# Merging two first-layer matmuls into one of 512 columns in 51 product pairs, and three more splits per chunk on GpSimd

## The chip, the core and the metric

One core of a Trainium2 chip runs the whole program. Its engines run side by side, each through its own queue in order, and wait for each other by semaphores: TensorE (PE in the profile; its weight loads are PEld), VectorE (DVE), ScalarE (ACT), GpSimd (POOL) and SyncE (SP), which issues nearly all transfers. The metric is the time of one execution in microseconds (us) on the device; lower is better. Matmuls read SBUF and write PSUM; a bank of PSUM holds 512 float32 columns.

## The reference

```python
# attention per batch and head (8 x 8), 576 tokens, head size 64, 128 random features
q_p, k_p = phi(q * scale), phi(k * scale)     # exp(x @ omega.T - |x|^2/2 - max) / sqrt(128)
x = (q_p @ (k_p.T @ v)) / (q_p @ k_p.sum(0) + 1e-6)   # then heads side by side: 8 x 576 x 512
# token mixing and MLP
u = x + mix(x)                                # x.T @ U @ V over the 576 tokens, rank 32
out = u + np.maximum(u @ w_ch1, 0.0) @ w_ch2  # 512 -> 2048 -> 512
```

Nothing is rounded on purpose: the result is asked for in the precision of float32. The change lies in the last line alone, in `u @ w_ch1`.

## The kernel before

**Stages.** Attention and mixing fill the first 400 us or so. Then comes the MLP over 4608 tokens, which are 36 tiles of 128. They are taken in nine chunks (`c`): chunk 0 has six tiles, chunks 1 to 7 have four (512 tokens), chunk 8 has two. Chunks 0 and 8 go through `whole1`, a plain matrix product, and the change does not touch them.

**Pairs.** In chunks 1 to 7 the first layer is computed in eight pairs (`p` = 0 to 7). Pair `p` makes two column blocks of `u @ w1`, `p` and `p + 8`, 128 columns each, for 512 tokens. Weights and tokens are cut into 2 x 2 blocks (halves of the 512 inputs; two column blocks, two halves of 256 tokens), and the 2 x 2 product is made with seven block products in place of eight, from sums and differences of the blocks. `products` issues them in the order (X, Y, Z, X, Y, W, Z), which names the PSUM bank that each accumulates into: product 3 goes on top of product 0 in X, product 4 on top of 1 in Y, product 6 on top of 2 in Z. So a bank has to be read between its two products. The text counts products from 0 to 6.

**High and low parts.** Matmuls run on `fp32r`, and each operand is kept as a high part and the rest (`split`: ACT casts the high part, another engine subtracts it). A product of 256 inputs is two steps `k` of 128, and each step three passes: high weights by high tokens, high weights by low tokens, low weights by high tokens. That is 7 x 2 x 3 = 42 matmuls of 256 columns a pair (L958).

**What reads them.** `after(i)` issues, after product i, what turns the banks into the hidden layer. `sums` is one DVE step (L771). Before the change: after product 0, ACT copies X to `p1` (L935); after 1, `u2 = Y + p1`; after 3, `relu` of X; after 4, `u3 = Y + p1`, then `c22 = Z + u3` and its `relu`; after 5, `c21 = W + u3` and its `relu`; after 6, `c12 = Z + u2` and its `relu`. `relu` is one ACT step for the high part of `g` (L916) and one DVE step for the low part (L918). The tiles are called `near` (`p1`, `u2`, `u3`, `c21`) and `far` (`c22`, `c12`) in the profile, the banks `p_s`.

**The second layer in between.** The 24 matmuls of 512 columns that take a pair's `g` into the output (L984, `second`) are handed out one at a time by `take` between the first-layer matmuls of the next pair: one between two products (`between`), two inside products 1, 3 and 5 and three inside the others. Results of a chunk are added to `u` and stored by `store` (DVE L1005, then SP) from `between`, one after each product, in the first pair of the next chunk.

**The next chunk.** In pairs 5 and 6 DVE transposes the tokens of the next chunk (L855), GpSimd makes their sums (L872, tile `us`), and in pair 7 `Chunk.add` splits the seven operands (L767 ACT, L768 the rest; tiles `ux`, `uy`): the first ahead of the pair, the others after products 0 to 5, DVE subtracting except for operands 3 and 5 of chunk 1. In chunk 1 the pairs also make the weight operands of the pairs that follow, from sums on DVE (`ws`) and splits on ACT and GpSimd (`wx`); from chunk 2 on these are read back from memory.

Names such as `keep` hold each engine's queue to the order of the program text.

## Time and profile before

| | |
|---|---|
| median of 3 runs | 1090.22 us (1090.05 to 1092.08) |
| profiled execution | 1088.64 us, of it the span of the core's instructions 1086.9 us |
| granted TensorE clock, mean | 0.996 |
| busy | PE 99%, PEld 90%, DVE 61%, ACT 46%, POOL 31% |
| chain that ended last | PE 84%, DVE 5%, ACT 3%, issue 2%, POOL 2% |
| L958, first-layer matmuls | 1728 + 624 |
| L984, second-layer matmuls | 1728 |

The page gives busy time by engine, the span in 40 slices, the chain of work that ended last, and groups of equal instructions with the mean time of one. A matmul's duration in the rows contains time in which the next one already runs, so what a matmul costs is read from one start to the next.

```profile
PE   9999999999999999999999999999999999999998
DVE  4689998998977776655733634634643643643421
POOL 3247547556445556565200100100100100100143
```

These are tenths of busy time in 40 slices of 27 us: the pairs of chunks 2 to 7 lie in about slices 20 to 38, where DVE has room and POOL has little to do.

### The profile page before, as it was taken

Reading aid. Unit: us, or ns where it says so; the run is one execution under the profiler, and the core shown is the slowest. Engines: PE = TensorE matmul, PEld = TensorE weight load, DVE = VectorE, ACT = ScalarE, POOL = GpSimd, SP = SyncE. Lnnn points to the kernel's source line nnn. Section 1 sums busy time; section 2 is a strip of 40 time slices with the busy share of each in tenths; the row PEclk is TensorE's granted clock in tenths of the full one; section 3 lists DMA queues with packets and bytes.
Section 4 is the critical chain, followed back from the end, with each engine's and each line's share of the span. In section 5 each row is a group of like instructions: output and inputs, shape, how many; then the busy total and the mean of one; then the engine's idle time right before and its main releaser. Section 6 shows DMA issues by size and latency. Waiting matters only on the chain.

```text
span 1086.9 us, 20562 instructions
## 1 busy us (share of the span) xinstructions
PE 1075.8 (99%) x7119; PEld 975.5 (90%) x7119; DVE 665.8 (61%) x1460; ACT 502.6 (46%) x1417; POOL 334.0 (31%) x345
## 2 busy tenths in 40 slices
PE   9999999999999999999999999999999999999998
PEld 8889999999988888898898989999888888888887
DVE  4689998998977776655733634634643643643421
ACT  5789989899856664343311312311321311311232
POOL 3247547556445556565200100100100100100143
PEclk9899999999999999999999999999999999999999
DMA  8688787787224453565776875875885785775510
GB/s 135 131 160 145 169 171 150 160 176 122 88 78 146 146 146 97 185 223 193 254 217 173 246 225 156 257 229 158 233 255 168 222 253 163 223 246 157 181 59 20
DMA packets 344583, 187.93 MB, mean 173 GB/s; under 512 B 276128, under 2 KB 276128, under 8 KB 344480
## 3 DMA queue, kind: packets, MB, share of 16 engines
q1 hardware_dynamic: 342112, 186.32, 63.3%
q8 instruction: 57, 0.93, 0.4%
q10 hardware_dynamic: 2368, 0.30, 0.2%
q14 instruction: 46, 0.38, 0.1%
HBM read 152.99 MB, written 33.55 MB: 172 GB/s over the span
## 4 chain that ended last, share of the span: by engine, by line
PE 84%; DVE 5%; ACT 3%; issue 2%; POOL 2%; DMA 1%; SPq 1%; POOLq 0%; DVEq 0%; ACTq 0%
PE p_s L958 25%; PE p_n L984 17%; PE p_q L984 15%; PE p_p L907 5%; PE p_n L494 4%; PE p_kv L448 4%; PE p_p L536 3%; PE p_p L537 2%; PE p_p L538 2%; PE p_q L474 2%; PE py L331 2%; POOL mag L168 1%; DVE mag L147 1%; ACT e L551 1%; DVE mag L144 1%
## 5 line engine op out<-in xcount | busy, mean ns | idle before, releaser
L958 PE MATMUL p_s<-ux,wx 128*128 128x256 f32 x1728 | 364.0, 280 | 0.4 <-DVE far L771 0.3
L958 PEld LDWEIGHTS p_s<-ux,wx 128*128 128x128 f32 x1728 | 321.6, 188 | 31.5 <-DVE far L771 0.6
L984 PE MATMUL p_n<-w2h,g 128*128 128x512 f32 x576 | 219.3, 395 | 0.0
L984 PE MATMUL p_q<-w2h,g 128*128 128x512 f32 x512 | 195.3, 392 | 0.0
L551 ACT ACTIVATE e<-p_p,nm 128x128 f32<-128x128 f32 x576 | 166.9, 389 | 25.0 <-DVE nm L544 16.3
L958 PE MATMUL p_s<-uy,wx 128*128 128x256 f32 x624 | 132.6, 279 | 0.0
L417 POOL TENSOR_TENSOR xl<-xT,xh 128x384 fp32r<-128x384 f32 x95 | 94.4, 1011 | 119.7 <-ACT xh L413 92.5
L958 PEld LDWEIGHTS p_s<-uy,wx 128*128 128x128 f32 x624 | 117.1, 188 | 11.1
L916 ACT ACTIVATE g<-far 128x256 fp32r<-128x256 f32 x112 | 46.8, 418 | 169.5 <-DVE far L771 169.5
L872 POOL TENSOR_TENSOR us<-uT 128x512 f32<-128x512 f32 x14 | 19.0, 1357 | 338.1 <-DVE uT L855 338.1
L984 PEld LDWEIGHTS p_n<-w2h,g 128*128 128x128 f32 x576 | 108.6, 189 | 9.3
L984 PE MATMUL p_n<-w2l,g 128*128 128x512 f32 x288 | 113.4, 394 | 0.0
L544 DVE TENSOR_REDUCE nm<-p_p 128x4 f32<-128x512 f32 x144 | 97.8, 679 | 25.1 <-PE p_p L538 17.1
L771 DVE TENSOR_TENSOR near<-p_s,near 128x256 f32<-128x256 f32 x168 | 70.4, 419 | 67.9 <-PE p_s L958 66.4
L768 POOL TENSOR_TENSOR wx<-w1f,wx 128x256 fp32r<-128x256 f32 x86 | 68.1, 807 | 135.2 <-DMA u<-u_dram 81.4
L918 DVE SCALAR_TENSOR_TENSOR g<-p_s,g 128x256 fp32r<-128x256 f32 x56 | 23.7, 423 | 138.6 <-ACT g L916 138.6
L916 ACT ACTIVATE g<-p_s 128x256 fp32r<-128x256 f32 x56 | 21.5, 383 | 184.8 <-PE p_s L958 184.8
L984 PEld LDWEIGHTS p_q<-w2h,g 128*128 128x128 f32 x512 | 96.2, 188 | 9.9
L984 PE MATMUL p_q<-w2l,g 128*128 128x512 f32 x256 | 100.7, 393 | 0.0
L536 PE MATMUL p_p<-omh,xh 128*128 128x256 f32 x288 | 93.2, 324 | 1.4 <-ACT e L551 0.9
L907 PE MATMUL p_p<-ux,wx 128*128 128x512 f32 (+1 forms) x480 | 84.5, 326 | 0.2 <-DVE g L918 0.2
L918 DVE SCALAR_TENSOR_TENSOR g<-far,g 128x256 fp32r<-128x256 f32 x112 | 49.5, 442 | 53.7 <-ACT g L916 53.7
(133 smaller groups left out, 2061.4 us busy)
## 6 DMA issues: line engine op xcount, KB each, us to landing
wx<-wx_dram SPq DMA_DIRECT2D x336, 256.0 KB, 3.2
raw<-in_moe_w_ch_dram SPq DMA_DIRECT2D x32, 512.0 KB, 4.0
wx_dram<-wx SPq DMA_DIRECT2D x56, 256.0 KB, 2.3
u_dram<-x SPq DMA_DIRECT2D x36, 256.0 KB, 2.1
u<-u_dram SPq DMA_DIRECT2D x34, 256.0 KB, 4.2
out_dram<-u SPq DMA_DIRECT2D x34, 256.0 KB, 3.2
kt<-in_k_dram SPq DMA_DIRECT2D x120, 72.0 KB, 2.7
qt<-in_q_dram SPq DMA_DIRECT2D x120, 72.0 KB, 2.6
```

Source lines behind the costliest of these rows:

```text
L417: rest.tensor_tensor(out=self.xl[-1], in0=self.turned, in1=f32(self.xh[-1]), op=ALU.subtract)
L448: tc.keep_in_program_order(nc.tensor.matmul(o, e[:, h, :], w, start=(s == 0 and h == 0), stop=(s == NT - 1), skip_group_check=True))
L536: nc.tensor.matmul(o, part.xh[g][:, ts], oh, start=True, stop=False)
L544: nc.vector.tensor_reduce(out=self.nm[:, :n], in_=self.pp[:, :n], axis=AX.X, op=ALU.max, negate=True)
L551: nc.scalar.activation(out=self.e[:, j, :], in_=self.pp[:, j, :], func=AF.Exp, bias=self.nm[:, j : j + 1])
L768: keep(rest.tensor_tensor(out=hl[:, 1], in0=x, in1=f32(hl[:, 0]), op=SUBTRACT))
L771: keep(nc.vector.tensor_tensor(out=out, in0=a, in1=b, op=op))
L907: nc.tensor.matmul(ph, l, r, start=(cc + i == 0), stop=(cc == NC - 1 and i == 2))
L916: keep(nc.scalar.activation(out=g[:, 0, ts], in_=x, func=AF.Relu))
L918: keep(nc.vector.scalar_tensor_tensor(out=g[:, 1, ts], in0=x, scalar=0.0, in1=f32(g[:, 0, ts]), op0=ALU.max, op1=ALU.subtract))
L958: tc.keep_in_program_order(nc.tensor.matmul(o, l, r, start=(i in (0, 1, 2, 5) and k + j == 0), stop=(k == 1 and j == 2), skip_group_check= ...
L984: tc.keep_in_program_order(nc.tensor.matmul(po, l, r, start=(begin and n + i == 0), stop=(end and n == len(fs) - 1 and i == 2)))
```

## The change

In 51 pairs (all eight of chunks 2 to 7, and pairs 2, 3 and 4 of chunk 1; `wide`), the first two passes of each step, which share the high weights, become one matmul whose moving operand is the high and the low tokens side by side: 2 x 256 = 512 columns. The bank is then two halves wide, and the second half holds the product with the low tokens. The third pass goes on top of the first half. A step is two matmuls in place of three, a pair 28 in place of 42. The two halves have to be added: where one instruction read a bank, `whole` and `add` now use one for the first half and a DVE sum for the second. After product 3, `c21` serves as a scratch tile for X. Second-layer matmuls stand at other places inside a product, in the same number.

The other edit moves the subtraction of operands 1, 3 and 5 of chunks 2 to 7 from DVE to GpSimd (chunk 1's 3 and 5 were there already).

```diff
-            split(self.slot(self.ops), x, nc.gpsimd if self.c == 1 and i in (3, 5) else nc.vector)
+            split(self.slot(self.ops), x, nc.gpsimd if i in ((3, 5) if self.c == 1 else (1, 3, 5)) else nc.vector)
...
-            bank = lambda n, b: ps.tile([P, HT], F32, name="p_s", tag=n, bufs=b)
+            bank = lambda n, b: ps.tile([P, 1 + wide, HT], F32, name="p_s", tag=n, bufs=b)
...
+            def whole(to, o):
+                keep(nc.scalar.copy(out=to, in_=o[:, 0]))
+                if wide:
+                    sums(to, o[:, 1], to, ADD)
+
+            def add(to, o, x):
+                sums(to, o[:, 0], x, ADD)
+                if wide:
+                    sums(to, o[:, 1], to, ADD)
...
                 if i == 0:
-                    keep(nc.scalar.copy(out=p1, in_=X))
+                    whole(p1, X)
                 elif i == 1:
-                    sums(u2, Y, p1, ADD)
+                    add(u2, Y, p1)
                 elif i == 3:
-                    self.relu(g[0], t1, X)
+                    if wide:
+                        whole(c21, X)
+                    self.relu(g[0], t1, c21 if wide else X[:, 0])
                 elif i == 4:
                     out()
-                    sums(u3, Y, p1, ADD)
-                    sums(c22, Z, u3, ADD)
+                    add(u3, Y, p1)
+                    add(c22, Z, u3)
                     self.relu(g[1], t2, c22, out)
                 elif i == 5:
-                    sums(c21, W, u3, ADD)
+                    add(c21, W, u3)
                     self.relu(g[1], t1, c21)
                 elif i == 6:
-                    sums(c12, Z, u2, ADD)
+                    add(c12, Z, u2)
                     self.relu(g[0], t2, c12)
...
+                    parts = [(o[:, 0], *lr) for lr in passes((wt[:, 0, k], wt[:, 1, k]), (x[:, 0, k], x[:, 1, k]))]
+                    if wide:
+                        parts[:2] = [(o, wt[:, 0, k], x[:, :, k])]
...
-                        if 3 * k + j in ((1, 3) if i % 2 else (0, 2, 3)):
+                        if n in (((1, 2), (0, 1, 2)) if wide else ((1, 3), (0, 2, 3)))[i % 2 == 0]:
                             take(steps, 1)
...
-            g = now.products(pairs, between, steps, out)
+            g = now.products(pairs, between, steps, out, c > 1 or 1 < p < 5)
```

In the changed kernel the first-layer matmuls are L972, the second layer L999, the copy L934, and `store` L1020.

**TensorE, from the end of product 4 to the start of product 6** in the second pair of chunk 4 (`uy` is the operand of product 4, `ux` that of 5 and 6; `w2h`, `w2l` are second-layer weights). Before:

```order
L958 MATMUL p_s<-uy,wx 128x256 x2
L984 MATMUL p_q<-w2h_5703,g 128x512
L958 MATMUL p_s<-ux,wx 128x256 x2
L984 MATMUL p_q<-w2h_77,g 128x512
L958 MATMUL p_s<-ux,wx 128x256 x2
L984 MATMUL p_q<-w2l_78,g 128x512
L958 MATMUL p_s<-ux,wx 128x256 x2
L984 MATMUL p_q<-w2h_77,g 128x512
L958 MATMUL p_s<-ux,wx 128x256
```

Now:

```order
L972 MATMUL p_s<-uy,wx 128x256
L999 MATMUL p_q<-w2h_5703,g 128x512
L972 MATMUL p_s<-ux,wx 128x512
L972 MATMUL p_s<-ux,wx 128x256
L999 MATMUL p_q<-w2h_77,g 128x512
L972 MATMUL p_s<-ux,wx 128x512
L999 MATMUL p_q<-w2l_78,g 128x512
L972 MATMUL p_s<-ux,wx 128x256
L999 MATMUL p_q<-w2h_77,g 128x512
L972 MATMUL p_s<-ux,wx 128x512
```

Between product 4 and product 6 there stand the same four second-layer matmuls and product 5, now as two matmuls of 512 and two of 256 columns. The last row of each is product 6's first matmul, into Z.

**VectorE, in any pair of chunks 2 to 7 without stores or transposes**, from product 3 to product 5. Before:

```order
L918 SCALAR_TENSOR_TENSOR g<-p_s,g 128x256
L771 TENSOR_TENSOR near<-p_s,near 128x256
L771 TENSOR_TENSOR far<-p_s,near 128x256
L918 SCALAR_TENSOR_TENSOR g<-far,g 128x256
L771 TENSOR_TENSOR near<-p_s,near 128x256
```

Now, from the four sums `p1`, `u2` (two) and `c21` on, whose last is the one after product 3:

```order
L771 TENSOR_TENSOR near<-p_s,near 128x256 x4
L918 SCALAR_TENSOR_TENSOR g<-near,g 128x256
L771 TENSOR_TENSOR near<-p_s,near 128x256 x2
L771 TENSOR_TENSOR far<-p_s,near 128x256
L771 TENSOR_TENSOR far<-p_s,far 128x256
L918 SCALAR_TENSOR_TENSOR g<-far,g 128x256
```

Between the low part of `g` after product 3 and the last read of Z there were two sums and now there are four; the low part of `g` itself now follows a sum and not PSUM alone. On ScalarE one COPY of X stands ahead of the ReLU after product 3.

**GpSimd, from one chunk's sums to the next one's** (the row `us<-uT` follows the transposes in pair 5 or 6; the second `us<-uT,us` is made in pair 7). Before:

```order
L872 TENSOR_TENSOR us<-uT 128x512
L872 TENSOR_TENSOR us<-uT,us 128x512
L872 TENSOR_TENSOR us<-uT 128x512
L872 TENSOR_TENSOR us<-uT,us 128x512
L872 TENSOR_TENSOR us<-uT 128x512
```

Now:

```order
L872 TENSOR_TENSOR us<-uT 128x512
L872 TENSOR_TENSOR us<-uT,us 128x512
L872 TENSOR_TENSOR us<-uT 128x512
L768 TENSOR_TENSOR ux<-us,ux 128x512
L872 TENSOR_TENSOR us<-uT,us 128x512
L768 TENSOR_TENSOR ux<-uT,ux 128x512
L768 TENSOR_TENSOR uy<-us,uy 128x512
```

In pair 7 the low parts of operands 1, 3 and 5 now stand around the sum that follows operand 1; on VectorE the same three rows are gone from that pair. SP's queue is the same but for line numbers.

## The prediction, made before the change was run

> **What bounds the kernel now.** I read the head of the page first, then the table of stretches for the product stage, then who waited for whom on TensorE, and last single rows of the timeline.

> ```profile
> span 1086.9 us, 20562 instructions
> PE 1075.8 (99%) x7119; PEld 975.5 (90%) x7119; DVE 665.8 (61%) x1460; ACT 502.6 (46%) x1417; POOL 334.0 (31%) x345
> 530.00:1030.00 500.00, 500.00 (x3144) 449.84 (x3143) 237.25 (x515) 114.57 (x279) 29.94 (x24) 1.00 0.71 212
> PE p_s L958 <- DVE far L771: 0.3, 1, 0.3
> ```

> TensorE (PE) is busy 99% of the span. The third line is the stretch that holds chunks 2 to 7, 48 of the 51 changed pairs (busy us and count of PE, its weight loads, DVE, ACT, POOL, then the clock): PE is busy 500.00 of 500.00 us at clock 1.00, VectorE (DVE) 237, ScalarE (ACT) 115, GpSimd (POOL) 30. The last line is all that PE waited from 500 to 1033 us: once. So nothing hides behind PE here; every wait put on it is paid in full, and each step off it is gained in full. The sum is made against the profiled execution, 1088.64 us (span 1086.9 and 1.74 around it); the median of the runs is 1.6 higher. A move under 0.2% (2 us) can't be told from none.

> **Part 1, the matmuls.** Each of the 714 merges (51 pairs, 14 each) turns two matmuls of 256 columns, which share their weights, into one of 512. Rows of PE, start and duration:

> ```profile
> 427.01 0.39 PE L984 MATMUL p_m<-w2h,g 128*128 128x512 f32 x1
> ...
> 428.37 4.32 PE L907 MATMUL p_p<-ux,wx 128*128 128x512 f32 x24
> ...
> 1039.24 0.88 PE L907 MATMUL p_p<-uy,wx 128*128 128x256 f32 x6
> 1039.95 0.88 PE L907 MATMUL p_p<-ux,wx 128*128 128x256 f32 x6
> 1040.67 0.40 PE L984 MATMUL p_n<-w2h,g 128*128 128x512 f32 x1
> ```

> The durations overlap, so the price is start to start. Six of 512 columns lie between the first two rows: 1.36/6 = 0.227 us. Twelve of 256 lie in the last three: 1.43/12 = 0.119. Inside a pair, below, a 512 takes 0.23 and two 256 take 0.23 to 0.24. A merge so saves 0.001 to 0.011 us; no row shows a moving operand in two strided halves, so these are its bounds too. I take 0.005, nearer the rows inside a pair: 714 x 0.005 = 3.6 us gained (0.7 to 7.9).

> [...]

> **Part 2, the additional sums.** Each product now leaves two halves. Per wide pair that is one more ACT copy and seven more DVE sums. DVE has room on average (237 of 500), so what counts is order. Product 6 accumulates into Z, so its first matmul has to wait until DVE has read product 2 out of Z, and this read stands behind all of product 4's sums. A normal pair now (chunk 4, second pair), PE, then DVE, then ACT:

> ```profile
> 712.45 0.40 PE L958 MATMUL p_s<-uy,wx 128*128 128x256 f32 x2
> 712.69 0.40 PE L984 MATMUL p_q<-w2l,g 128*128 128x512 f32 x1
> ...
> 714.08 0.40 PE L958 MATMUL p_s<-uy,wx 128*128 128x256 f32 x2
> 714.32 0.40 PE L984 MATMUL p_q<-w2h,g 128*128 128x512 f32 x1
> ...
> 715.95 0.28 PE L958 MATMUL p_s<-ux,wx 128*128 128x256 f32 x1
> ```

> ```profile
> 713.36 0.42 DVE L918 SCALAR_TENSOR_TENSOR g<-p_s,g 128x256 fp32r<-128x256 f32 x1 [3.00 <-ACT g L916]
> 714.51 0.42 DVE L771 TENSOR_TENSOR near<-p_s,near 128x256 f32<-128x256 f32 x1 [0.73 <-PE p_s L958]
> 714.97 0.42 DVE L771 TENSOR_TENSOR far<-p_s,near 128x256 f32<-128x256 f32 x1
> 715.88 0.42 DVE L918 SCALAR_TENSOR_TENSOR g<-far,g 128x256 fp32r<-128x256 f32 x1 [0.48 <-ACT g L916]
> 716.22 0.42 DVE L771 TENSOR_TENSOR near<-p_s,near 128x256 f32<-128x256 f32 x1
> ```

> ```profile
> 712.95 0.38 ACT L916 ACTIVATE g<-p_s 128x256 fp32r<-128x256 f32 x1 [4.12 <-PE p_s L958]
> 715.43 0.42 ACT L916 ACTIVATE g<-far 128x256 fp32r<-128x256 f32 x1 [2.10 <-DVE far L771]
> 718.96 0.37 ACT L935 COPY near<-p_s 128x256 f32<-128x256 f32 x1 [0.54 <-PE p_s L958]
> ```

> Product 3 ends at 712.45 + 0.40 = 712.85, product 4 at 714.48, product 6 starts at 715.95, 3.10 after product 3's end. DVE reads Z at 714.97 and is done at 715.39: 0.56 us to spare today. A DVE step that needs the one before starts 0.46 after it (714.51, 714.97); one that doesn't, 0.34 after it (715.88, 716.22); a step handed from one engine to another starts 0.03 to 0.04 after the end.

> The new chain from product 3's end: ACT copies c21's first half (0.37) 0.04 to 0.41; DVE adds the second (0.42) 0.44 to 0.86; ACT's ReLU (0.42) 0.90 to 1.32; DVE's low part of g starts at 1.35, so u3's first sum at 1.69 (matmuls of product 4 are done by 1.63); then four sums in a chain: 1.69 + 3 x 0.46 = 3.07 for the last, which ends at 3.49. PE gets there at 3.10 less four merges, 3.08. Such a wait stands in the trace once, in the last pair of chunk 1:

> ```profile
> 526.16 0.40 PE L984 MATMUL p_q<-w2h,g 128*128 128x512 f32 x1
> 526.82 0.39 PE L958 MATMUL p_s<-ux,wx 128*128 128x256 f32 x1 [0.27 <-DVE far L771]
> 527.04 0.40 PE L984 MATMUL p_q<-w2h,g 128*128 128x512 f32 x1
> ...
> 526.34 0.42 DVE L771 TENSOR_TENSOR far<-p_s,near 128x256 f32<-128x256 f32 x1
> ```

> DVE ends at 526.76, the matmul starts 0.05 later, and the next one comes 0.22 after it in place of 0.12: 0.10 lost to the restart. So PE starts at 3.54 against 3.08 and pays 0.46 + 0.10 = **0.56 us a pair**. Bounds: 0.35, if the restart costs no 0.10 and each link is a little shorter; 0.66, if ACT's copy starts 0.10 after the matmul as the ReLU at 712.95 does. Behind it the work of products 5 and 6 slips by as much as PE does, so I count no second wait. The other reuses have room: X is read twice before product 3, Y before product 4, each over a microsecond ahead. It is paid in 37 pairs (six in each of chunks 2 to 7, and the last of chunk 7): 20.7 us.

> In the first pair of chunks 2 to 7 the stores of the chunk before stand in the same queue, one ahead of u3:

> ```profile
> 706.97 0.68 DVE L1005 TENSOR_TENSOR u<-p_q,u 128x512 f32<-128x512 f32 x1
> 707.57 0.41 DVE L771 TENSOR_TENSOR far<-p_s,near 128x256 f32<-128x256 f32 x1
> ```

> A store holds DVE 0.60 (706.97 to 707.57): 6 x (0.56 + 0.60) = 7.0 us. Here DVE's 0.60 had the 0.56 of slack as cover; the four sums used that cover up.

> **Part 3, GpSimd.** Three of the seven low parts of the next chunk go from DVE to POOL: 18 in all, off a queue that is late and onto one that idles (30 of 500 us). First single steps of today's last pair of chunk 2, then groups of the page (busy us, mean ns of one):

> ```profile
> 605.29 0.69 DVE L768 TENSOR_TENSOR ux<-us,ux 128x512 fp32r<-128x512 f32 x1
> ...
> 606.23 1.67 DVE L768 TENSOR_TENSOR uy<-us,uy 128x512 fp32r<-128x512 f32 x1
> ...
> 606.06 1.30 POOL L872 TENSOR_TENSOR us<-uT,us 128x512 f32<-128x512 f32 x1 [1.74 <-DVE ux L768]
> ...
> L918 DVE SCALAR_TENSOR_TENSOR g<-near,g 128x256 fp32r<-128x256 f32 x56 | 29.1, 520 | 27.1 <-ACT g L916 27.1
> L767 ACT CAST ux<-us 128x512 fp32r<-128x512 f32 x20 | 11.9, 616 | 0.1
> L771 DVE TENSOR_TENSOR ws<-w1f 128x256 f32<-128x256 f32 x16 | 8.4, 523 | 0.0
> L768 POOL TENSOR_TENSOR ux<-us,ux 128x512 fp32r<-128x512 f32 x1 | 1.7, 1742 | 0.0
> ```

> The rows show a price: the same DVE subtraction of two SBUF operands took 0.69 alone and 1.67 while POOL's 1.30 ran. In the last pair of chunks 2 to 6 POOL now does three of up to 1.74 and one sum of 1.30 besides, 5.2 to 6.5 us of some 12, while DVE does eight steps of this kind (four low parts, four of g). Without meeting: operand 4's low part stands ahead of u3 and needs ACT's 0.62 cast after the ReLU, to 1.94; DVE starts it at 1.97, u3 follows 0.60 later at 2.57 and not 1.69: 0.56 + 0.88 = 1.4 us. With three low parts caught at 0.98 each, 4.3. I take 3.0, in between, since POOL is at work about half the time: 5 x 3.0 = 15.0 us. In the three wide pairs of chunk 1 weight sums (L771 `ws`, 0.52 mean) stand in DVE's queue, and POOL works on weights: 0.56, one sum more (0.40), half of the g steps longer by up to 0.5 (mean 0.52 against 0.42): 3 x 1.4 = 4.2 us (0.6 to 2.0 each). The wait at 526.82 should go, as its pair loses three DVE subtractions: 0.5 us gained.

> No DMA and no store changes its place in SP's queue, so I cost them at nothing: a longer pair only gives the weight tiles' transfers more time to land.

> **Sum.** 20.7 + 7.0 + 15.0 + 4.2 - 0.5 - 3.6 = +42.8 us on 1088.64: 1131.4, and 1133 on the scale of the median.

> **Rivals.**
> - *POOL's parts don't meet DVE's.* The last pairs cost 1.4, those of chunk 1 0.9: 20.7 + 7.0 + 7.0 + 2.7 - 4.1 = 33.3, 1123.5 us. For it: 13 of these subtractions ran at 0.69. Chance 0.16.
> - *They meet throughout and the delay runs on to products 3 and 4*: 4.3 and 2.0 each, +51.1, 1141 us. For it: the row at 606.23. Chance 0.20. [...]
> - *The normal pair's wait is covered*, because I have a link or two too many, and only the queues of first, last and chunk 1 pairs cost: 3.6 + 12.2 + 2.5 - 4.1 = 14.2, 1104 us. Against it: the single row at 526.82 waits in just this place. Chance 0.05.
> - *Faster: nothing waits.* Then only -4.1 is left, 1086 us. It needs the chain of 3.49 to end by 3.03, two of its links gone. Chance 0.03.
> - *Faster: the pairs are paced by weight loads.* PEld is busy 450 of 500 us, and 14 of 66 loads a pair go. At 500/3144 = 0.159 us each that is 113 us: 1024 us. It decides the sign from 0.065 us saved a merge (46.4/714); the rows give 0.011 at most. Chance 0.02. [...]

> **Chances.** The main case has 0.52; 0.02 is left for sums that end within 0.2% by accident. Faster 0.05, same 0.02, slower 0.93. The bounds of all terms give 1109 to 1149; the range 1114 to 1146 takes in the first two rivals and leaves out under 2 in 10.

> **What would show it.** PE's waits: some 50 of `p_s` (now L972) on DVE `far`, 0.4 to 0.5 us each in normal pairs, and L972 PE rows of 512 columns that start 0.23 before the next. A normal pair lasts some 11.0 us in place of 10.5. In last pairs POOL rows `ux<-us,ux` beside DVE rows over 1 us. Wrong if PE's table of waits stays near empty, if the next matmul after a merged one comes under 0.2 us later, or if the waits stand at product 3 or in the second layer.

## The result and the profile after

The changed kernel takes 1135.07 us (median of 4 runs, 1134.84 to 1135.94) beside 1090.13 us for the kernel before (4 runs): 4.25% slower, ratio 1.0425 [1.0407, 1.0443], 44.9 us. The profiled execution of the changed kernel is the one of 1135.94 us.

The page of the changed kernel, its head and TensorE's row of 40 slices; then the stretch 530 to 1075 us (busy us and count of PE, PEld, DVE, ACT, POOL, then the granted clock, DMA share and GB/s); then what PE and its weight loads waited for (us in total, times, longest):

```profile
span 1134.1 us, 19646 instructions
PE 1092.5 (96%) x6405; PEld 944.9 (83%) x6405; DVE 789.1 (70%) x1799; ACT 520.5 (46%) x1468; POOL 359.4 (32%) x363
PE   9989999999999999999999999899899999999998
```

```profile
530.00:1075.00 545.00, 519.47 (x2494) 424.31 (x2493) 354.75 (x834) 131.37 (x328) 51.60 (x39) 0.99 0.67 197
```

```profile
PE p_s L972 <- DVE far L771: 27.7, 51, 2.0
```

PE has 714 instructions less and was busy all the time before; now it idles 25.5 of 545 us there. In the table of waits one short row has become 51 waits, one for each wide pair, 27.7 us in all. All are of the kind that stood once in the trace before, and all stand ahead of product 6: its first matmul (L972) waits for the last DVE sum into `far`, the read of bank Z. DVE is busy 355 of 545 us and is nowhere near full; it is late in one place of every pair. The clock reads 0.99 over a stretch in which it read 1.00 before; that comes below.

A normal pair (chunk 4, second pair) from the timeline: PE, then ACT, then DVE.

```profile
732.25 0.28 PE L972 MATMUL p_s<-uy,wx 128*128 128x256 f32 x1
...
735.26 0.28 PE L972 MATMUL p_s<-ux,wx 128*128 128x256 f32 x1
735.39 0.40 PE L999 MATMUL p_q<-w2h,g 128*128 128x512 f32 x1
736.07 0.50 PE L972 MATMUL p_s<-ux,wx 128*128 128x512 f32 x1 [0.28 <-DVE far L771]
736.40 0.40 PE L999 MATMUL p_q<-w2h,g 128*128 128x512 f32 x1
```

```profile
732.56 0.37 ACT L934 COPY near<-p_s 128x256 f32<-128x256 f32 x1 [2.84 <-PE p_s L972]
733.43 0.42 ACT L916 ACTIVATE g<-near 128x256 fp32r<-128x256 f32 x1 [0.49 <-DVE near L771]
```

```profile
732.97 0.42 DVE L771 TENSOR_TENSOR near<-p_s,near 128x256 f32<-128x256 f32 x1 [1.13 <-ACT near L934]
733.88 0.42 DVE L918 SCALAR_TENSOR_TENSOR g<-near,g 128x256 fp32r<-128x256 f32 x1 [0.48 <-ACT g L916]
734.22 0.88 DVE L771 TENSOR_TENSOR near<-p_s,near 128x256 f32<-128x256 f32 x2
735.13 0.42 DVE L771 TENSOR_TENSOR far<-p_s,near 128x256 f32<-128x256 f32 x1
735.59 0.42 DVE L771 TENSOR_TENSOR far<-p_s,far 128x256 f32<-128x256 f32 x1
```

Product 3 ends at 732.25 + 0.28 = 732.53. From there every link is to be seen: copy, sum, ReLU, low part, the two sums of u3, the two of c22, the last of which ends at 736.01, 3.48 later. PE had been free to start product 6 at 735.39 + 0.23 = 735.62 and starts at 736.07. That is 0.45 of waiting; the 0.28 in brackets is less, because the row's end of the matmul before lies inside the next one's time. The matmul after it comes 0.33 later and not 0.23: 0.10 for the restart.

Pair by pair, from the starts of PE's rows in both traces (lost is what a start comes later than 0.23 us behind a matmul of 512 columns or 0.118 behind one of 256):

| | predicted | measured |
|---|---|---|
| 37 normal pairs | 20.7 | 20.6 (0.556 each) |
| 6 first pairs | 7.0 | 6.9 (1.155 each) |
| 5 last pairs, chunks 2 to 6 | 15.0 | 11.4 (2.27 each) |
| 3 wide pairs of chunk 1 | 4.2 | 2.7 (0.894 each) |
| last pair of chunk 1 | -0.5 | -0.5 |
| half clock, 4 times | none | 6.2 (1.55 each) |
| 714 merges | -3.6 | -2.0 |
| sum | 42.8 | 45.3 |

Read directly, from the first pair's first matmul to the last first-layer matmul, the stage grew from 587.3 to 632.5 us, 45.1; the sum agrees to 0.2. The row of the merges is no reading of its own: it is what a pair lost less what it grew by (0.556 less 0.516 in a normal pair). The two profiled executions differ by 47.3; 2.2 of it lies ahead of chunk 1, where both kernels are the same (its first matmul starts at 447.05 and 444.89 us), and the medians differ by 44.9.

The row that nobody foresaw is the clock. The last pair of chunk 3, PE rows of the timeline, then the stretches around it:

```profile
709.54 0.39 PE L999 MATMUL p_q<-w2h,g 128*128 128x512 f32 x1
711.91 0.70 PE L972 MATMUL p_s<-ux,wx 128*128 128x512 f32 x1 [1.99 <-DVE far L771]
...
713.48 0.63 PE L972 MATMUL p_s<-ux,wx 128*128 128x512 f32 x1
713.90 0.63 PE L999 MATMUL p_q<-w2h,g 128*128 128x512 f32 x1
714.33 0.84 PE L972 MATMUL p_s<-ux,wx 128*128 128x256 f32 x2
```

```profile
702.90:712.05 9.15, 7.16 (x36) 5.75 (x35) 7.40 (x14) 4.21 (x10) 4.82 (x4) 1.00 0.70 188
712.05:715.46 3.41, 3.41 (x10) 2.75 (x11) 2.52 (x6) 1.69 (x4) 1.28 (x1) 0.50 1.05 307
715.46:725.00 9.54, 8.72 (x44) 7.07 (x42) 5.88 (x14) 1.58 (x4) 0.00 (x0) 1.00 0.67 184
```

PE starts nothing between 709.54 and 711.91. At 712.05 the granted clock falls to 0.50 for 3.41 us: matmuls of 512 columns start 0.42 to 0.43 apart. Then it is whole again. The same stands after the last pairs of chunks 4, 5 and 6 (from 804.21, 896.37 and 988.53), and not after that of chunk 2, whose gap is as long (2.40 from 619.08).

### The profile page after: what moved, and what is told of

Its sections match the earlier page's. It is cut to its first block, busy times and chain, and to the rows that moved or that the text cites. A ratio compares the mean times of both kernels' runs of the same rounds, so it can differ in the third digit from the quotient of the medians.

```text
span 1134.1 us, 19646 instructions
## 1 busy us (share of the span) xinstructions
PE 1092.5 (96%) x6405; PEld 944.9 (83%) x6405; DVE 789.1 (70%) x1799; ACT 520.5 (46%) x1468; POOL 359.4 (32%) x363
## 4 chain that ended last, share of the span: by engine, by line
PE 73%; DVE 13%; ACT 6%; SPq 3%; issue 3%; DMA 1%; POOL 0%; POOLq 0%; DVEq 0%; ACTq 0%
PE p_s L972 19%; PE p_n L999 18%; PE p_p L907 8%; PE p_q L999 7%; DVE near L771 5%; DVE far L771 4%; PE p_n L494 4%; PE p_kv L448 3%; SPq L575 3%; PE p_p L536 2%; PE p_p L537 2%; PE p_p L538 2%; PE p_q L474 2%; ACT g L916 2%; DVE g L918 2%
## 5 line engine op out<-in xcount | busy, mean ns | idle before, releaser
L972 PE MATMUL p_s<-ux,wx 128*128 128x256 f32 (+1 forms) x1202 | 369.8, 336 | 20.3 <-DVE far L771 20.2
L972 PEld LDWEIGHTS p_s<-ux,wx 128*128 128x128 f32 x1202 | 227.2, 190 | 61.0 <-DVE far L771 31.4
L771 DVE TENSOR_TENSOR near<-p_s,near 128x256 f32<-128x256 f32 x423 | 177.3, 419 | 95.8 <-ACT near L934 83.8
L999 PE MATMUL p_n<-w2h,g 128*128 128x512 f32 x576 | 216.8, 395 | 0.0
L999 PE MATMUL p_q<-w2h,g 128*128 128x512 f32 x512 | 197.4, 396 | 0.0
L972 PE MATMUL p_s<-uy,wx 128*128 128x256 f32 (+1 forms) x436 | 134.5, 334 | 7.5 <-DVE far L771 7.5
L916 ACT ACTIVATE g<-far 128x256 fp32r<-128x256 f32 x112 | 46.8, 418 | 203.7 <-DVE far L771 203.7
L999 PEld LDWEIGHTS p_n<-w2h,g 128*128 128x128 f32 x576 | 109.0, 189 | 20.6
L872 POOL TENSOR_TENSOR us<-uT 128x512 f32<-128x512 f32 x14 | 19.1, 1362 | 334.7 <-DVE uT L855 334.7
L999 PE MATMUL p_n<-w2l,g 128*128 128x512 f32 x288 | 114.0, 396 | 0.0
L999 PEld LDWEIGHTS p_q<-w2h,g 128*128 128x128 f32 x512 | 96.8, 189 | 18.9
L768 POOL TENSOR_TENSOR wx<-w1f,wx 128x256 fp32r<-128x256 f32 x86 | 68.0, 806 | 134.4 <-DMA u<-u_dram 82.3
L934 ACT COPY near<-p_s 128x256 f32<-128x256 f32 x107 | 39.1, 366 | 147.6 <-PE p_s L972 147.3
L999 PE MATMUL p_q<-w2l,g 128*128 128x512 f32 x256 | 101.4, 396 | 0.0
L972 PEld LDWEIGHTS p_s<-uy,wx 128*128 128x128 f32 x436 | 82.0, 188 | 22.5 <-DVE far L771 12.6
L916 ACT ACTIVATE g<-near 128x256 fp32r<-128x256 f32 x107 | 44.7, 418 | 99.4 <-DVE near L771 99.4
L918 DVE SCALAR_TENSOR_TENSOR g<-near,g 128x256 fp32r<-128x256 f32 x107 | 51.8, 484 | 51.8 <-ACT g L916 51.8
L918 DVE SCALAR_TENSOR_TENSOR g<-far,g 128x256 fp32r<-128x256 f32 x112 | 48.5, 433 | 53.7 <-ACT g L916 53.7
```

The source lines that it names most:

```text
L768: keep(rest.tensor_tensor(out=hl[:, 1], in0=x, in1=f32(hl[:, 0]), op=SUBTRACT))
L771: keep(nc.vector.tensor_tensor(out=out, in0=a, in1=b, op=op))
L916: keep(nc.scalar.activation(out=g[:, 0, ts], in_=x, func=AF.Relu))
L918: keep(nc.vector.scalar_tensor_tensor(out=g[:, 1, ts], in0=x, scalar=0.0, in1=f32(g[:, 0, ts]), op0=ALU.max, op1=ALU.subtract))
L972: tc.keep_in_program_order(nc.tensor.matmul(to, l, r, start=(i in (0, 1, 2, 5) and k + j == 0), stop=(k == 1 and j == len(parts) - 1), ski ...
L999: tc.keep_in_program_order(nc.tensor.matmul(po, l, r, start=(begin and n + i == 0), stop=(end and n == len(fs) - 1 and i == 2)))
```

## The experiments

Eight kernels were run. "Normal", "first" and "last" pairs are those of the prediction; lost times are read as in the table above.

**merge_only: the merging alone, without the three splits on GpSimd.** Edit against the changed kernel:

```diff
-            split(self.slot(self.ops), x, nc.gpsimd if i in ((3, 5) if self.c == 1 else (1, 3, 5)) else nc.vector)
+            split(self.slot(self.ops), x, nc.gpsimd if self.c == 1 and i in (3, 5) else nc.vector)
```

> The merging without the three further splits on GpSimd (DVE keeps them, as before the change). Theory (the wait of product 6 for DVE's read of Z): normal pairs keep their 0.56 us wait; the last pairs have three more DVE subtractions of 0.60 to 0.69 us in the queue but none that runs into GpSimd's splits: within 7 us of the changed kernel, 1128 to 1142. Rival (GpSimd's splits do most of the harm in the last and first pairs of a chunk, where after shows 2.3 to 3.3 and 1.2 to 2.2 us of lost time): those eleven pairs fall to 1.4 and 1.2 us, 12 us less: about 1123.

1137.2 us, ratio 1.0436 [1.0416, 1.0456]; the changed kernel's interval overlaps. Normal pairs lose 0.56 to 0.57, last pairs 2.44 (2.33 of waiting), and the half clock comes after all five (a mean of 0.98 over 530 to 1075 us). The wait of the last pair of chunk 1 is there again (0.52). PE's waits:

```profile
PE p_s L972 <- DVE far L771: 28.9, 52, 2.2
```

So the loss is the merging's, and the splits on GpSimd give back 0.17 a last pair, not more: what DVE no longer does is nearly made up for by what GpSimd does to DVE.

**pool_only: the splits on GpSimd alone, without merging.** Edit against the kernel before:

```diff
-            split(self.slot(self.ops), x, nc.gpsimd if self.c == 1 and i in (3, 5) else nc.vector)
+            split(self.slot(self.ops), x, nc.gpsimd if i in ((3, 5) if self.c == 1 else (1, 3, 5)) else nc.vector)
```

> The three further splits on GpSimd alone, no merging. Theory: with 0.56 us of slack before product 6 they cost nothing, and the one wait of before (last pair of chunk 1, 0.54 us) goes: 1089.5, no change that can be told. Rival (they hurt by themselves): a microsecond or more in each of six last pairs, 1096 or more.

1089.88 us, ratio 1.0 [0.999, 1.0009]: no difference. PE is busy without a break, at full clock:

```profile
530.00:1075.00 545.00, 545.00 (x3425) 489.75 (x3424) 240.96 (x521) 128.92 (x322) 69.56 (x65) 1.00 0.67 197
```

**early_z: the same merging, but Z is read early.** Right after product 2 the bank is copied to c22, and after product 4 c22 takes u3 on top. The number of DVE steps stays the same, ACT makes one copy more a pair; what changes is the release of Z. Edit against the changed kernel:

```diff
+                elif i == 2 and wide:
+                    whole(c22, Z)
...
-                    add(c22, Z, u3)
+                    sums(c22, c22 if wide else Z[:, 0], u3, ADD)
```

> The changed kernel, but Z is read right after product 2 (ACT copies the first half into c22, DVE adds the second), and after product 4 c22 gets u3 added in SBUF: one DVE sum and one read of Z fewer stand behind product 4, and product 6 waits for no sum of products 3 and 4. Same merges, same number of DVE sums, one ACT copy more a pair. Theory: the 37 normal pairs lose their wait whole (20.6 us), the first and last pairs of a chunk keep part of theirs, since DVE is short there: 1100 to 1112. Rival (the merged matmul itself is what costs): stays over 1130.

1099.69 us, ratio 1.0091 [1.0076, 1.0107], just under the 1100 to 1112 expected: 35 of the 45 us are gone, the half clock with them (1.00 over 530 to 1075 us). Most normal pairs, from the third of a chunk on, last 10.44 us with no wait at all, 0.06 less than before the change. The waits that are left:

```profile
PE p_n L1001 <- ACT g L916: 4.5, 5, 0.9
PE p_s L974 <- issue: 0.9, 5, 0.2
PE p_s L974 <- DMA wx<-wx_dram: 0.4, 1, 0.4
```

This is the test of the cause: the same matmuls and the same number of DVE sums, and the wait ahead of product 6 goes when the read of Z is taken out of the chain. What remains lies mainly at the start of chunks 3 to 7 (1.5 us more than before in each first pair, 0.4 to 1.0 in each second): the work of the pair before arrives late. In the first pairs the second layer waits for `g` (0.9 in the table, 1.06 from start to start). And a wait on Z is left there, now at product 2, which opens the bank anew; the table puts it down to `issue`. First pair of chunk 3, DVE's last read of Z in the pair before and product 2's first matmul:

```profile
616.62 0.42 DVE L771 TENSOR_TENSOR far<-p_s,far 128x256 f32<-128x256 f32 x1
617.15 0.47 PE L974 MATMUL p_s<-uy,wx 128*128 128x512 f32 x1 [0.18 <-issue]
```

In each of the ten first and second pairs of chunks 3 to 7 this matmul starts 0.10 after the end of that read.

**before_repeat: the kernel before, with two sums done twice.** No merging; in the 51 pairs u3 and c22 are summed twice, so that DVE's queue grows by two steps ahead of Z's release and by nothing else:

```diff
-                    sums(u3, Y, p1, ADD)
-                    sums(c22, Z, u3, ADD)
+                    for _ in range(2 if c_wide else 1):
+                        sums(u3, Y, p1, ADD)
+                    for _ in range(2 if c_wide else 1):
+                        sums(c22, Z, u3, ADD)
```

> The kernel before, no merging and no move to GpSimd; in the same 51 pairs the two sums after product 4 are each done twice (u3 again, c22 again: same values). Theory: two links of 0.46 us more use up the 0.51 us that DVE had before product 6, so PE waits 0.41 us and loses 0.10 us to the restart: 51 x 0.51 = 26 us, and the first and last pairs of a chunk pay their stores and splits besides (about 0.6 us each, 7 us): 1112 to 1126. Rival (merged matmuls or full banks cost, not the queue): 1090, unchanged.

1118.15 us, ratio 1.026 [1.0246, 1.0274]. Normal pairs lose 0.526 (0.42 of waiting, 0.105 of restart), last pairs 0.743, and first pairs 0.526: the store's 0.60 that the changed kernel pays, and that was expected here too, does not show.

```profile
PE p_s L960 <- DVE far L771: 14.3, 52, 0.5
```

Two DVE steps of this queue make nearly the whole wait of a normal pair, without a merged matmul or a wider bank. Why the store is free there can be read from the kernel before, first pair of chunk 4, DVE:

```profile
703.20 0.68 DVE L1005 TENSOR_TENSOR u<-p_n,u 128x512 f32<-128x512 f32 x1
704.01 0.42 DVE L771 TENSOR_TENSOR near<-p_s,near 128x256 f32<-128x256 f32 x1
```

The store holds DVE until 0.60 after its start (as from 706.97 to 707.57), 703.80, and u3 follows only at 704.01: without a chain over c21 the low part of `g` comes early (702.86), and u3 waits for product 4 anyway, whose last two matmuls (703.58, 0.40) end at 703.98. In the changed kernel u3 follows the low part at once (733.88, 734.22 above), so a store between them is paid in full.

**halves_unmerged: the changed kernel with its merged matmul taken apart** into two of 256 columns, one for each half of the bank, all sums as in the changed kernel:

```diff
-                        parts[:2] = [(o, wt[:, 0, k], x[:, :, k])]
+                        parts[1] = (o[:, 1], *parts[1][1:])
...
-                            to, l, r, start=(i in (0, 1, 2, 5) and k + j == 0), stop=(k == 1 and j == len(parts) - 1),
+                            to, l, r, start=(i in (0, 1, 2, 5) and k == 0 and (j == 0 or wide and j == 1)), stop=(k == 1 and j == len(parts) - 1),
...
-                        if n in (((1, 2), (0, 1, 2)) if wide else ((1, 3), (0, 2, 3)))[i % 2 == 0]:
+                        if n in ((1, 3), (0, 2, 3))[i % 2 == 0]:
```

Both halves' first matmuls now carry `start`, and the kernel leaves part of the sums out (which part, no run here shows); every matmul is issued all the same.

> The changed kernel with the two-halved banks, all sums and copies and the GpSimd splits, but the merged matmul taken apart again: high weights by high tokens into the first half, by low tokens into the second, 256 columns each, 42 matmuls a pair. Theory (the sums behind product 4 cost, a merge is worth 0.004 us): the waits stay, and of 14 merges a pair the four of products 4 and 5 lie under the wait: 51 x 10 x 0.004 = 2 us over the changed kernel, 1136 to 1139. Rival (the matmul of 512 columns with a strided operand is what costs): 1090 to 1110.

1138.51 us, ratio 1.0439 [1.0417, 1.0461]. Its 5 runs reach from 1133.51 to 1139.82, and its profiled execution, the fastest of them, has the half clock after three of the five last pairs (0.99 over 530 to 1075 us), so the median does not settle a matter of 3 us. Its pairs do: a normal pair is 0.571 longer than in the kernel before, against 0.516 in the changed kernel, one of chunk 1 0.922 against 0.869. The 14 merges of a pair so save about 0.055 us, 0.004 each, 2.8 us in 51 pairs (2.0 against the kernel before). Four of them, in products 4 and 5, lie under the wait, so these are low figures; the next run has no wait. The waits are the same with and without merged matmuls (0.55 a normal pair), since they come from the sums.

**early_z_30, merging where DVE has room:** Z read early, merging only in pairs 1 to 5 of chunks 2 to 7 (30 pairs, away from the queues of first and last pairs), and the additional splits on GpSimd only for chunk 2's operands, which the last pair of chunk 1 makes. Edit against the changed kernel, beside the early read:

```diff
-            split(self.slot(self.ops), x, nc.gpsimd if i in ((3, 5) if self.c == 1 else (1, 3, 5)) else nc.vector)
+            split(self.slot(self.ops), x, nc.gpsimd if i in {1: (3, 5), 2: (1, 3, 5)}.get(self.c, ()) else nc.vector)
...
-            g = now.products(pairs, between, steps, out, c > 1 or 1 < p < 5)
+            g = now.products(pairs, between, steps, out, c > 1 and 0 < p < 6)
```

> The early read of Z, merged only in the pairs that have DVE to spare: pairs 1 to 5 of chunks 2 to 7 (30 pairs); GpSimd takes the three further splits for chunk 2 alone, where before waited once. Theory: 10.44 us a pair in place of 10.50 (as in the run with the early read), no wait in the 30 pairs: 30 x 0.06 = 1.8 us gained and the 0.54 us of the one wait: 1087.4, a ratio of 0.998. Rival (the delay of DVE moves on into the pairs that follow, as first pairs did): 1092 or more.

1087.88 us (12 runs) beside 1090.35 (17 runs), ratio 0.9984 [0.9973, 0.9996]. PE does not stop after 430 us:

```profile
530.00:1075.00 545.00, 545.00 (x3016) 471.52 (x3015) 326.20 (x747) 150.41 (x384) 50.07 (x52) 1.00 0.68 197
```

The 30 pairs are 1.8 us shorter together (0.06 each, 0.004 a merge), the other pairs of these chunks 0.2 longer, and the wait of 0.5 in the last pair of chunk 1 is gone. The interval lies just below 1: a gain of about 0.2%. An estimate for all 51 pairs, if none waited, is 51 x 0.06 = 3 us; this is what the merging has to give.

**wait_ladder: gaps of several lengths, for the clock.** The kernel before, u3's sum repeated 3 to 10 times in pairs 2 and 4 of chunks 2 to 7, which makes gaps of 1.1 to 4.3 us in PE:

```diff
-                    sums(u3, Y, p1, ADD)
+                    for _ in range(1 + more):
+                        sums(u3, Y, p1, ADD)
```

> The kernel before with u3's sum repeated in two pairs of each of chunks 2 to 7, 3 to 10 times, so that product 6 waits for a known time: extra sums x 0.46 - 0.51 us, that is 0.87, 1.33 (chunk 2), 1.8, 2.2 (3), 2.2, 2.7 (4), 2.7, 3.2 (5), 3.2, 3.6 (6) and 4.1, 1.8 (7), 30 us in all. In the changed kernel four of five waits that left 2.4 us between two matmul starts were followed by 3.4 us at half the granted clock, and 0.6 to 1.2 us never. Theory (a wait above some 2 us can drop the clock, by where it falls in a fixed grid of 3.4 us): none after 1.8 us or less, after some of 2.2 to 3.2, after all over 3.4; each drop costs 1.7 us more: 1120 to 1135. Rival (the drop has another cause, such as the load on the chip): no drops at all.

One run, 1127.7 us; what counts are its gaps. Two gaps of the same length, PE rows, and the 3.41 us behind each:

```profile
667.15 0.40 PE L985 MATMUL p_q<-w2h,g 128*128 128x512 f32 x1
669.64 0.39 PE L959 MATMUL p_s<-ux,wx 128*128 128x256 f32 x1 [2.09 <-DVE far L771]
...
734.08 0.40 PE L985 MATMUL p_q<-w2h,g 128*128 128x512 f32 x1
736.56 0.39 PE L959 MATMUL p_s<-ux,wx 128*128 128x256 f32 x1 [2.09 <-DVE far L771]
```

```profile
669.89:673.30 3.41, 3.41 (x14) 3.02 (x14) 1.61 (x4) 0.98 (x3) 0.00 (x0) 0.50 0.00 0
...
738.15:741.56 3.41, 3.41 (x23) 3.06 (x23) 1.57 (x4) 0.84 (x3) 0.00 (x0) 1.00 0.45 137
```

The first gap of 2.48 us halves the clock, the second doesn't. The starts of all drops in this trace (669.89, 826.90, 919.06, 942.95, 1014.63) lie whole multiples of 3.413 us apart: 46, 27, 7 and 21. If that grid is laid through the trace, the gap from 667.15 falls into one cell, with 2.25 us of idle in it (counted from 0.23 after the last matmul's start), and the one from 734.08 is cut by a cell's edge into 0.43 and 1.82 (the shortest gap, 1.11 from 557.8, was followed by no drop and is left out):

| gap at | start to start, us | most idle in one cell, us | half clock |
|---|---|---|---|
| 579.8, 644.3, 1036.4 | 1.57, 2.03, 2.03 | 1.09, 1.48, 1.80 | no |
| 734.1, 757.5, 848.7 | 2.48, 2.94, 3.40 | 1.82, 1.77, 1.90 | no |
| 667.2, 823.3, 914.8 | 2.48, 2.94, 3.40 | 2.25, 2.71, 2.59 | yes |
| 940.6, 1009.7 | 3.87, 4.32 | 2.08, 2.76 | yes (the first for two cells, 6.83 us) |

The changed kernel fits: its four gaps with a drop have 2.14 to 2.15 us in one cell, the one without has 1.59. In these traces, then, not the length of a gap decides but how much of it falls into one cell: 2.08 us and more was followed by half clock, 1.90 and less was not.

**low_on_act: the low parts of the three operands on ACT.** In chunks 2 to 7 neither GpSimd nor DVE makes them; ACT copies the operand in place of the difference:

```diff
-            split(self.slot(self.ops), x, nc.gpsimd if i in ((3, 5) if self.c == 1 else (1, 3, 5)) else nc.vector)
+            split(self.slot(self.ops), x, (nc.gpsimd if i in (3, 5) else nc.vector) if self.c == 1 else nc.scalar if i in (1, 3, 5) else nc.vector)
...
+        if rest is nc.scalar:
+            keep(nc.scalar.copy(out=hl[:, 1], in_=x))
```

> The changed kernel with the low parts of operands 1, 3 and 5 of chunks 2 to 7 not subtracted on GpSimd: ACT copies the operand there instead (so these low parts are not the true ones). It tells what GpSimd's splits cost DVE in the last pairs. Theory (two-operand DVE steps that meet a GpSimd step are held up by 0.5 to 1.0 us): the wait of the last pairs falls from 2.15 to about 1.3 us, the clock does not drop in the pairs after, so 5 x 0.85 + 4 x 1.7 = 11 us less: about 1124. Rival (the queue alone makes the wait): 2.0 us and more stay, 1133 to 1136.

1124.94 us, ratio 1.0322 [1.0302, 1.0343]. Last pairs lose 1.62 in place of 2.27, their gaps are 1.69 long, and no clock drop follows (1.00 over 530 to 1075 us). PE's waits:

```profile
PE p_s L975 <- DVE far L774: 24.1, 51, 1.3
```

The two kernels so differ by 0.65 us a last pair (3.3 in all). By the starts of the pairs the changed kernel is 9.6 us longer than this one: 3.3 and the four drops, 6.2, make 9.5. This is the run that ties the clock to the gaps in time as well: gaps below 2 us, no drop, and its price gone from the time. The meeting itself in the changed kernel, last pair of chunk 3, POOL and DVE, and then DVE in low_on_act at the same place:

```profile
707.98 1.29 POOL L768 TENSOR_TENSOR uy<-uT,uy 128x512 fp32r<-128x512 f32 x1
```

```profile
708.04 1.51 DVE L918 SCALAR_TENSOR_TENSOR g<-near,g 128x256 fp32r<-128x256 f32 x1 [0.48 <-ACT g L916]
709.47 0.68 DVE L768 TENSOR_TENSOR uy<-us,uy 128x512 fp32r<-128x512 f32 x1
710.07 0.87 DVE L771 TENSOR_TENSOR near<-p_s,near 128x256 f32<-128x256 f32 x2
```

```profile
707.53 0.43 DVE L921 SCALAR_TENSOR_TENSOR g<-near,g 128x256 fp32r<-128x256 f32 x1 [0.48 <-ACT g L919]
708.04 0.69 DVE L771 TENSOR_TENSOR uy<-us,uy 128x512 fp32r<-128x512 f32 x1
708.65 0.88 DVE L774 TENSOR_TENSOR near<-p_s,near 128x256 f32<-128x256 f32 x2
```

A step of 0.43 takes 1.51 and ends 0.28 after POOL's; the subtraction behind it, with POOL idle, takes 0.68. In all five last pairs it is this low part of `g`, after product 3, that meets GpSimd's second split, and it takes 1.50 to 1.53 each time; in the pair shown the first split is over before product 3 ends, and the third starts after product 6 has begun. From the start of that low part to u3 (`near`) it takes 2.03 us in the changed kernel and 1.12 here. So the meeting costs 0.9; the two kernels differ by 0.65 only, because ACT's three copies have a price as well: they hold up the copy of X, and from product 3's end to the low part it takes 1.58 here and 1.35 in the changed kernel.

## Why the prediction came out right, and where it was off

1133.0 was forecast and 1135.07 measured, +42.8 beside +44.9; but errors of opposite signs stand behind this agreement.

- *The normal pair, 0.56 us.* Right in place, mechanism and size: 0.556, with the chain 3.48 long (3.49 predicted) and PE there after 3.09 (3.08). That early_z loses nothing in most of them and before_repeat loses 0.526 without any merging shows that the wait is Z's release behind DVE's queue.
- *First pairs, 0.56 + 0.60.* Right: 1.155. DVE's store starts 0.60 before u3. But the row at 706.97 that I showed for it stands ahead of c12, not of u3, and in the kernel before slack did not cover the store ahead of u3: u3 waited for product 4 anyway (704.01, above).
- *Last pairs, 3.0 taken from between 1.4 and 4.3.* Too high: 2.27. The step that failed is the price of GpSimd: I put 1.6 a pair on the meetings, and they cost 0.9 by the rows. GpSimd's split took 1.30 and not the 1.74 that I read from a single row, and one of g's low parts was caught in each of these pairs, not three steps. The lower end, without a meeting, was 1.4; low_on_act has 1.62, of which 0.23 are ACT's copies.
- *Chunk 1, 1.4.* Too high, by the same error: 0.894. One weight sum stands ahead of u3 (0.34), the wait of 0.556 is the rest, and g's low parts there take 0.42, so GpSimd did not lengthen them.
- *The wait of 0.5 in the last pair of chunk 1.* Gone, as predicted. It is gone in pool_only too, so it is the splits that remove it, as argued.
- *The merges, 0.005 each.* 0.003 to 0.004, within the bounds; 2.0 to 3.0 us and not 3.6.
- *Nothing behind the waits.* Wrong: the half clock, 6.2 us, was missed altogether. I priced a gap at its length plus 0.10. With last pairs of 3.0 as I had them, gaps of over 2 us stood in my own sum, and the question what the clock does in them was not asked.

So 5.1 us too much (last pairs and chunk 1) stand against 6.2 (clock) and 1.6 (merges) too little. Of the rivals, the first (GpSimd's parts don't meet DVE's, 1123.5) is nearly what low_on_act makes of the kernel, 1124.94, with ACT's copies in it; the second (they meet throughout and hold up products 3 and 4, 1141) is not seen, since all 51 waits are on `far`, none at products 3 and 4. The covered normal pair and both faster ones are excluded by the 51 waits.

What stays open: the exact amount of idle that halves the clock (in merge_only a cell with 1.99 us was enough, in halves_unmerged one with 2.02 was not, so either it is not one fixed number or the count of the idle time is a little rough), and the small waits of second pairs in early_z beside the one on Z. That the second split on GpSimd makes the loss of a last pair is read from the rows; the three were not taken away one by one.

## What to carry to other kernels

An accumulator bank is free when its last reader is done (here the next writer started 0.05 to 0.10 us after it), so before adding readers, follow the chain from the last event that they depend on to the bank's next writer, link by link with the trace's durations; an engine that is busy 65% of the time (355 of 545 us) can be late in every round. If a read holds a bank, copy it out early to a scratch tile and add there: that took away 35 of 45 us here at an unchanged number of matmuls. What it frees can move the wait to the bank's next opening, as at product 2 here. And keep TensorE's gaps under some 2 us, since a longer one may be paid a second time in clock (1.55 us a drop here).
